# Keys and values loaded by pairs of batch rows, in a one-core decode block

## The chip, the cores and the metric

The kernel runs on one core of a Trainium2 chip. The metric is the device time of one execution in microseconds (us); lower is better. The traces are taken by the hardware profiler in one execution.

## The reference

One decode step (one token for each of 4 batch rows) of a transformer block: layer norm, attention over the last W = 2048 positions of a key and value cache, a residual, a second layer norm and a gated feed-forward network. All tensors are bf16.

```python
B, D, F = 4, 1024, 3584
Hq, Hkv, Sk, Dh = 32, 4, 8192, 128        # 8 query heads share one key head
W = min(4096, max(256, Sk // 4))          # 2048

def _A_ref(x, k_cache, v_cache, wq, wo):
    q = (x @ wq).reshape(B, 1, Hq, Dh).transpose(0, 2, 1, 3)
    k = jnp.repeat(k_cache[:, :, Sk - W:, :], 8, axis=1)
    v = jnp.repeat(v_cache[:, :, Sk - W:, :], 8, axis=1)
    scores = jnp.einsum("bhqd,bhkd->bhqk", q, k) * (Dh ** -0.5)
    p = _softmax(scores, axis=-1)
    o = jnp.einsum("bhqk,bhkd->bhqd", p, v)
    return o.transpose(0, 2, 1, 3).reshape(B, 1, Hq * Dh) @ wo

def _B_ref(x, w1, w3, w2):
    return (_silu(x @ w1) * (x @ w3)) @ w2

h = x + _A_ref(_layernorm(x), k_cache, v_cache, wq, wo)
return h + _B_ref(_layernorm(h), w1, w3, w2)
```

## The kernel before

**The ring.** All weights, keys and values live in one SBUF tile, `ring`, of five units of 16384 elements per partition. wq takes units 0 and 1; the keys `k_s` units 3 and 4; the values of batch rows 0 and 1 unit 2, and of rows 2 and 3 unit 0, after wq. wo takes units 3 and 4 after the keys; w1 starts at unit 1 and reaches into unit 2, over the values; w3 starts at unit 3, over wo; the parts of w2 take unit 0 and then unit 1. Each load is one `dma_start` on SP's queue (`load`, line 124). SP issues in program order, and a load that reuses space waits until the last instruction that reads the overlapped bytes is done. The order is wq in three parts, keys, values, wo, w1, w3, w2 in five parts.

**Keys and values.** A row of the cache tensor is split over partitions: each of 32 pieces of 64 positions of each of the 4 key heads takes one partition, so a load of one batch row is 2 MB in rows of 16 KB per partition (`k_v`, line 75). There are four such loads for keys and four for values.

**Scores.** `transpose_k` turns the 64 blocks of 128x128 of one batch row on TensorE (line 267, PE), 16 at a time into PSUM, and copies them back over the keys, on VectorE (line 269, DVE) and ScalarE (line 271, ACT) in turn. `scores` (line 290) multiplies 32 query columns with 512 keys at a time, four such matmuls side by side in four column groups of the array, 16 per batch row. The keys of one head are every fourth column of the transposed blocks; that is the step of `kT` (line 285).

**Softmax and output.** `row_max` and `bias_of` give the maxima for a pair of batch rows, `softmax` (line 331) the exponentials on ACT, [128, 512] for each row. `spread` (line 344) multiplies each probability with a mask of four columns, one for each key head (`gmask`), so that a probability stands in the column of its head and zeros in the other three; `transpose_p` (line 366) transposes the 128x2048 result on DVE in 32x32 blocks into `PT`; `output` (line 381) multiplies it with the values in 16 matmuls that each take four blocks, and keeps the right parts with `jmask` (`od`, line 389); two additions on GpSimd (POOL, lines 398 and 399) follow. After the last row the outputs are gathered (`on_ps`, line 441; `oP`, line 448) and multiplied with wo (`y_ps`, line 468).

**The rest.** The second layer norm follows, `up_projection` of w1 (`gate`, line 492), the reciprocal for silu (line 513), `up_projection` of w3 (`up`), and two stages with w2 (lines 533 and 548).

The program's order is written out by hand (`manual_schedule`), so on each engine the instructions run in the order of the text.

Of the kernel before, what the change touches and what calls it, by code (L numbers as in the profile page):

```python
# [10 lines left out]
P = 128  # L11
# [3 lines left out]
BF16 = mybir.dt.bfloat16  # L15
FP32 = mybir.dt.float32
# [5 lines left out]
def kernel(  # L22
# [20 lines left out]
    nc = tc.nc  # L43

    B, _, D = A_x.shape
    Hkv, Sk, Dh = A_k_cache.shape[1], A_k_cache.shape[2], A_k_cache.shape[3]
# [3 lines left out]
    W = min(4096, max(256, Sk // 4))  # L50
# [4 lines left out]
    C = 4  # L55
    R = 32
    S = R // B
    DQ = D // C
# [7 lines left out]
    x_flat = A_x.flatten_outer_dims()  # L66
    out_flat = out.flatten_outer_dims()
    wq_v = A_wq.rearrange("(p kc) n -> p kc n", kc=KC)
    T = NQ // P
    JR = W // R  # L70
    L5 = R // Hkv
    JB = 16
    JM = 4

    k_v, v_v = (
        a[:, :, Sk - W : Sk, :].rearrange("b g (i j) d -> i g b (j d)", j=JR)
        for a in (A_k_cache, A_v_cache)
    )
    wo_v = A_wo.rearrange("(p t) n -> p (t n)", t=T)
# [6 lines left out]
    ktpool = ctx.enter_context(tc.tile_pool(name="ktpool", bufs=2))  # L86
    ptpool = ctx.enter_context(tc.tile_pool(name="ptpool", bufs=3))
    stream = ctx.enter_context(tc.tile_pool(name="stream", bufs=1))
    ps = ctx.enter_context(tc.tile_pool(name="ps", bufs=1, space=bass.MemoryType.PSUM))
# [8 lines left out]
    def at(unit, *shape):  # L98
        o = unit * UNIT
        view = ring[:, o : o + int(np.prod(shape))]  # L100
        if len(shape) == 1:
            return view
        names = "abc"[: len(shape)]
        return view.rearrange(
            f"p ({' '.join(names)}) -> p {' '.join(names)}", **dict(zip(names, shape))
        )

    wq_s = at(0, KC, NQ)
    k_s = at(3, B, JR, Dh)
    v_s = [at((2, 0)[b // 2], 2, JR, Dh)[:, b % 2] for b in range(B)]  # L110
    wo_s = at(3, T, D)
    w1_s = at(1, KC, F)
    w3_s = at(3, KC, F)
# [2 lines left out]
    o = 0  # L116
    for i, n in enumerate(W2B):
        if i == 1:
            o = UNIT
# [3 lines left out]
    def load(dst, src):  # L123
        nc.sync.dma_start(out=dst, in_=src)

    def load_values(i):
        for b in (2 * i, 2 * i + 1):
            load(v_s[b].rearrange("p j d -> p (j d)"), v_v[:, :, b])

    ctx.enter_context(tc.manual_schedule())  # L130


    x_nat = act.tile([P, DQ], BF16)
    nc.gpsimd.memset(x_nat[:], 0.0)
    nc.scalar.dma_start(out=x_nat[::S, :], in_=x_flat.rearrange("b (c n) -> c b n", c=C))
    for r in (slice(0, 1), slice(1, KC // 2), slice(KC // 2, KC)):
        load(wq_s[:, r, :], wq_v[:, r, :])
    for b in range(B):
        load(k_s[:, b].rearrange("p j d -> p (j d)"), k_v[:, :, b])
    load_values(0)  # L140


# [15 lines left out]
        out=same[:], in_=t32[:].rearrange("p (o h) -> p o h", o=1).to_broadcast([P, C, R])  # L158
    )
    gmask = const.tile([P, 1, Hkv], BF16)  # L160
    with nc.allow_low_precision("sums of zeros and a single one"):
        nc.vector.tensor_reduce(
            out=gmask[:, 0], in_=t32[:].rearrange("p (g r) -> p g r", g=Hkv), axis=AX.X, op=ALU.add
# [3 lines left out]
    for j in range(JM):  # L167
# [3 lines left out]
        out=nscale[:], in_=ident_f[:2, :2], scalar=-qscale, op=ALU.mult  # L171
# [5 lines left out]
        out=place[:, : R * C].rearrange("p (h e) -> p h e", e=C)[:, :, C - 1], in_=t32[:]  # L177
# [6 lines left out]
        out=gather[:, :, :B], in_=ident[:].rearrange("p (c b s) -> p c b s", c=C, b=B)[:, :, :, 0]  # L184
# [44 lines left out]
    for kc in range(KC):  # L229
        for hf in range(2):  # L230
            for c in range(C):
                o = (2 * c + hf) * HALF * Dh
# [3 lines left out]
                    rhs=wq_s[:, kc, o : o + HALF * Dh],  # L236
                    start=(kc == 0),
                    stop=(kc == KC - 1),
# [6 lines left out]
    for r in range(REP):  # L245
# [8 lines left out]
        out=Qm[:].rearrange("p b (g y) -> p b g y", y=QW)[:, :, :, :REP],  # L254
        in_=qT_ps[:, :, :, :B].rearrange("p r g b -> p b g r"),
# [2 lines left out]

    n_step = 0

    def transpose_k(b, tags):
        nonlocal n_step
        for n in range(JR // JB):
            blocks = k_s[:, b, n * JB : (n + 1) * JB, :]
            kt_ps = ps.tile([P, JB, P], BF16, tag=tags[n_step % len(tags)], name="kt_ps")
            for jj in range(JB):
                nc.tensor.transpose(out=kt_ps[:, jj], in_=blocks[:, jj, :], identity=ident[:])  # L267
            if n_step % 2 == 0:
                nc.vector.tensor_copy(out=blocks, in_=kt_ps[:])  # L269
            else:  # L270
                nc.scalar.copy(out=blocks, in_=kt_ps[:])  # L271
            n_step += 1
# [4 lines left out]
    def scores_tile(i):  # L277
        sc_ps[i] = ps.tile([P, 2, W // C], FP32, tag=("scA", "scB")[i], name="sc_ps")
# [3 lines left out]
    om = act.tile([P, B, Dh], FP32)  # L282
    stage = {}

    kT = k_s.rearrange("p b j (q i g) -> p b g q j i", q=C, g=Hkv)

    def scores(b, gs):
        for g in gs:
            for q in range(C):
                nc.tensor.matmul(  # L290
                    sc_ps[b // 2][R * q : R * q + R, b % 2],
                    lhsT=Qm[:, b, g * R : (g + 1) * R],
                    rhs=kT[:, b, g, q],
                    start=(g == 0),
                    stop=(g == Hkv - 1),
                    tile_position=(0, R * q),
                )
# [40 lines left out]
        )  # L338
        stage[("p1", b)] = p1

    def spread(b):

        P4 = ktpool.tile([P, JR * L5, Hkv], BF16, tag="P4")
        nc.vector.tensor_tensor(  # L344
            out=P4[:],
            in0=stage.pop(("p1", b))[:].rearrange("p (x o) -> p x o", o=1).to_broadcast([P, JR * L5, Hkv]),
            in1=gmask[:].to_broadcast([P, JR * L5, Hkv]),
            op=ALU.mult,
        )
        stage[("P4", b)] = P4  # L350

    def total(i):

# [7 lines left out]
        )  # L361
        nc.vector.reciprocal(out=rinv[:, 2 * i : 2 * i + 2], in_=tot_ps)  # L362

    def transpose_p(b):
        PT = ptpool.tile([P, JR, R], BF16, tag="PT")
        nc.vector.transpose(  # L366
            out=PT[:].rearrange("p j h -> p (j h)"),
            in_=stage.pop(("P4", b))[:].rearrange("p x g -> p (x g)"),
        )
        stage[("PT", b)] = PT  # L370


    def output(b):
        PT = stage.pop(("PT", b))
        o_ps = (
            small[:, 0].rearrange("p (j d) -> p j d", j=JM)
            if b % 2
            else ps.tile([P, JM, Dh], FP32, tag="ktA", name="o_ps")[:]
        )
        for i in range(JR // JM):  # L380
            nc.tensor.matmul(  # L381
                o_ps,
                lhsT=PT[:, i * JM : (i + 1) * JM, :].rearrange("p j h -> p (j h)"),
                rhs=v_s[b][:, i * JM : (i + 1) * JM, :],
                start=(i == 0),
                stop=(i == JR // JM - 1),
            )
        od = act.tile([P, JM, Dh], FP32, tag="od", bufs=1)
        nc.vector.scalar_tensor_tensor(  # L389
            out=od[:],  # L390
            in0=o_ps,
            scalar=rinv[:, b : b + 1],
            in1=jmask[:].to_broadcast([P, JM, Dh]),
            op0=ALU.mult,
            op1=ALU.mult,
        )
        o2 = act.tile([P, 2, Dh], FP32, tag="o2", bufs=1)
        nc.gpsimd.tensor_tensor(out=o2[:], in0=od[:, :2], in1=od[:, 2:], op=ALU.add)  # L398
        nc.gpsimd.tensor_tensor(out=om[:, b], in0=o2[:, 0], in1=o2[:, 1], op=ALU.add)

    GS = range(Hkv)
    KT = ("ktA", "ktB", "scB")
    transpose_k(0, KT)
    transpose_k(1, KT)
    scores_tile(0)
    scores(0, GS)
    transpose_k(2, KT)
    scores(1, GS)
    transpose_k(3, KT)
    small = ps.tile([P, 2, 512], FP32, tag="ktB")  # L410
    scores_tile(1)
    scores(2, GS)
    row_max(0)
    scores(3, GS)
    bias_of(0)
    softmax(0)
    softmax(1)
    load(wo_s, wo_v.rearrange("p (t n) -> p t n", t=T))
    spread(0)
    row_max(1)  # L420
    transpose_p(0)
    bias_of(1)
    softmax(2)
    softmax(3)
    spread(1)
    transpose_p(1)
    total(0)
    output(0)
    spread(2)
    transpose_p(2)  # L430
    output(1)
    load(w1_s, w1_v)
    spread(3)
    transpose_p(3)
    total(1)
    output(2)
    output(3)

    on_ps = ps.tile([P, B, T], FP32, tag="scA")
    for e in range(C):  # L440
# [3 lines left out]
            rhs=om[:, :, e * T : (e + 1) * T],  # L444
            start=(e == 0),
            stop=(e == C - 1),
# [6 lines left out]
    for i in range(2):  # L453
        for k in range(2):
            c = i + 2 * k
# [3 lines left out]
                rhs=x_nat[:],  # L459
                start=(k == 0),  # L460
                stop=False,
# [3 lines left out]
    for t in range(T):  # L465
        row = wo_s[:, t].rearrange("p (k i n) -> p i k n", k=2, i=2)
        for i in range(2):
# [3 lines left out]
                rhs=row[:, i],  # L471
                start=False,
                stop=(t == T - 1),
# [34 lines left out]
    for w, n in zip(w2_s[1:], W2B[1:]):  # L508
# [8 lines left out]
        out=hg[:].rearrange("p (a f) -> p a f", a=2), in0=up_ps[:, :, :FH], in1=eg[:], op=ALU.mult  # L517
# [11 lines left out]
    for w, n in zip(w2_s[:NE], W2B[:NE]):  # L529
        for ff in range(n):  # L530
            row = w[:, ff].rearrange("p (k i n) -> p i k n", k=2, i=2)
            for i in range(2):
# [3 lines left out]
                    rhs=row[:, i],  # L536
                    start=(fc == 0),
                    stop=(fc == FE - 1),
# [6 lines left out]
    for w, n in zip(w2_s[NE:], W2B[NE:]):  # L545
        for ff in range(n):
            for c in range(C):
# [3 lines left out]
                    rhs=w[:, ff, c * DQ : (c + 1) * DQ],  # L551
                    start=(fc == FE),
                    stop=(fc == FC - 1),
# [5 lines left out]
    for i in range(2):  # L559
        for half, eng in enumerate((nc.sync, nc.scalar)):  # L560
            c = 2 * half + i
            eng.dma_start(
                out=out_flat[:, c * DQ : (c + 1) * DQ], in_=res[R * c : R * c + B, :]
# [31 lines left out]
```

## Time and profile before

| what | value |
|---|---|
| time, median of 3 runs | 139.23 us (139.12 to 139.4) |
| the profiled execution | 139.25 us |
| its span, first to last instruction | 137.2 us |
| PE, DVE, ACT, POOL busy | 55%, 36%, 21%, 11% of the span |
| SP's load queue | 55.58 MB, 95.0% of 16 DMA engines over the span |
| chain that ended last | DMA 60%, PE 27%, DVE 6%, ACT 3% |

Times are microseconds from the first instruction. PE is the matmul side of TensorE, PEld its weight loads; an engine's name with a q is its sequencer (SPq issues the loads). In a time line each row is: start, duration, engine, line, operation, output and inputs with shapes, count, and in brackets how long the engine was idle before and what ended it. In a list of waits: who waited for whom, the total, how often, the longest. "ring<-in_B_w_dram" is any of w1, w3 and w2. The page's row of DMA gives the busy tenths of the DMA engines in 40 equal slices of the span.

### The profile page before, as it was taken

What the parts mean: (1) busy time and instruction counts of PE and PEld (TensorE: products, weight loads), DVE (VectorE), ACT (ScalarE), POOL (GpSimd) and SP (SyncE); (2) the same over time, 40 slices, a digit from 0 to 9 for tenths busy, and PEclk for the clock granted to TensorE, in tenths of its full rate; (3) what the DMA queues carried; (4) which work ended last, traced back from release to release, by engine and by line L of the source; (5) the groups of instructions that cost most, each with busy time, mean ns of one, the idle gap of its engine ahead of it and who ended that gap; (6) DMA issues with size and microseconds to landing.
All of it is one profiled execution on the core that took longest, in us unless ns stands there. A gap on an engine that the chain in (4) does not pass through costs nothing.

```text
span 137.2 us, 1720 instructions
## 1 busy us (share of the span) xinstructions
PE 75.5 (55%) x744; PEld 41.4 (30%) x746; DVE 49.3 (36%) x47; ACT 28.5 (21%) x31; POOL 15.3 (11%) x41
## 2 busy tenths in 40 slices
PE   0002904689999983149938757971098000927450
PEld 0001301289875940033414314420043000404120
DVE  0012000016733563899699620023000297061021
ACT  3005000208949494022000000005001700000000
POOL 7304100000000000000358321002000000000000
PEclk9999995559999999555999999998556855699998
DMA  4999998999999999998979989969989899999950
GB/s 162 488 424 456 449 401 373 406 435 439 411 435 444 416 425 415 430 578 358 573 306 420 497 358 439 535 284 518 418 384 523 351 451 386 419 410 418 402 195 2
DMA packets 2795, 55.70 MB, mean 406 GB/s; under 512 B 324, under 2 KB 356, under 8 KB 612
## 3 DMA queue, kind: packets, MB, share of 16 engines
q1 hardware_dynamic: 2752, 55.58, 95.0%
q8 instruction: 6, 0.10, 0.3%
q10 hardware_dynamic: 36, 0.01, 0.0%
q14 instruction: 1, 0.01, 0.0%
HBM read 55.58 MB, written 0.01 MB: 405 GB/s over the span
## 4 chain that ended last, share of the span: by engine, by line
DMA 60%; PE 27%; DVE 6%; ACT 3%; issue 1%; SPq 1%; DVEq 0%
DMA ring<-in_B_w_dram 45%; DMA ring<-in_A_wq_dram 15%; PE kt_ps L267 9%; PE sc_ps L290 5%; PE o_ps L381 4%; PE gate L492 3%; PE q_ps L233 3%; DVE P L344 2%; DVE PT L366 2%; ACT ring L271 1%; PE small L381 1%; DVE ring L269 1%; DVE rmax L302 1%; PE qT_ps L246 1%; ACT q_sb L243 1%
## 5 line engine op out<-in xcount | busy, mean ns | idle before, releaser
L271 ACT COPY ring<-kt_ps 128x2048 bf16<-128x2048 bf16 x8 | 14.6, 1866 | 8.3 <-PE kt_ps L267 8.3
L267 PE MATMUL kt_ps<-ident,ring 128*128 128x128 bf16 x256 | 15.8, 225 | 0.6 <-DVE Qm L253 0.5
L267 PEld LDWEIGHTS <-ring 128*128 128x128 bf16 x256 | 15.3, 101 | 2.6 <-DMA ring<-in_A_k_cache_dram 1.7
L398 POOL TENSOR_TENSOR o<-od 128x256 f32<-128x256 f32 x4 | 6.8, 1696 | 59.7 <-DVE od L389 59.7
L269 DVE COPY ring<-kt_ps 128x2048 bf16<-128x2048 bf16 x8 | 9.8, 1225 | 10.1 <-PE kt_ps L267 10.1
L492 PEld LDWEIGHTS <-n_T 128*32 128x32 bf16 x128 | 4.7, 133 | 21.9 <-DMA ring<-in_B_w_dram 11.5
L233 PE MATMUL q_ps<-ring,n_T 128*32 128x512 bf16 x64 | 7.2, 627 | 7.2 <-DMA ring<-in_A_wq_dram 5.5
L513 DVE RECIPROCAL eg<-eg 128x896 f32<-128x896 f32 x1 | 5.8, 5753 | 13.2 <-ACT eg L512 13.2
L492 PE MATMUL up<-ring,n_T 128*32 128x448 bf16 x64 | 4.5, 452 | 10.8 <-DMA ring<-in_B_w_dram 10.8
L381 PEld LDWEIGHTS <-PT 128*128 128x128 bf16 x64 | 6.7, 108 | 9.2 <-issue 2.1
L344 DVE TENSOR_TENSOR P<-p,gmask 128x2048 bf16<-128x2048 bf16 x4 | 9.1, 2277 | 0.8 <-ACT p L331 0.8
L366 DVE STREAM_TRANSPOSE PT<-P 128x2048 bf16<-128x2048 bf16 x4 | 9.2, 2306 | 0.1
L492 PE MATMUL gate<-ring,n_T 128*32 128x448 bf16 x64 | 6.1, 574 | 5.5 <-DMA ring<-in_B_w_dram 5.5
L381 PE MATMUL o_ps<-ring,PT 128*128 128x512 bf16 x31 | 8.6, 431 | 0.2 <-issue 0.2
L193 PE MATMUL sums_ps<-both,mean_f 128*128 128x64 f32 x4 | 1.1, 367 | 13.0 <-ACT both L191 13.0
L290 PE MATMUL sc_ps<-ring,Qm 128*32 128x512 bf16 x64 | 7.6, 604 | 0.4 <-DVE ring L269 0.4
L533 PE MATMUL early_ps<-ring,hg_T 128*32 128x512 bf16 x42 | 4.9, 379 | 5.3 <-DMA ring<-in_B_w_dram 5.3
L381 PE MATMUL small<-ring,PT 128*128 128x512 bf16 x31 | 7.2, 379 | 0.7 <-DVE rinv L362 0.7
L468 PE MATMUL y_ps<-ring,oP 128*32 128x512 bf16 x64 | 7.1, 379 | 0.1
L233 PEld LDWEIGHTS <-n_T 128*32 128x32 bf16 x64 | 2.4, 139 | 11.2 <-issue 9.3
L253 DVE COPY Qm<-qT_ps 128x128 bf16<-128x128 bf16 x1 | 0.3, 292 | 15.0 <-PE qT_ps L246 15.0
L193 PEld LDWEIGHTS sums_ps<-both,mean_f 128*128 128x128 f32 x4 | 0.8, 250 | 13.5 <-issue 11.0
(77 smaller groups left out, 58.8 us busy)
## 6 DMA issues: line engine op xcount, KB each, us to landing
ring<-in_B_w_dram SPq DMA_DIRECT2D x2, 7168.0 KB
ring<-in_A_k_cache_dram SPq DMA_DIRECT2D x4, 2048.0 KB
ring<-in_A_v_cache_dram SPq DMA_DIRECT2D x4, 2048.0 KB, 43.0
ring<-in_A_wq_dram SPq DMA_DIRECT2D x1, 4096.0 KB, 20.7
ring<-in_B_w_dram SPq DMA_DIRECT2D x1, 3328.0 KB
ring<-in_A_wq_dram SPq DMA_DIRECT2D x1, 3072.0 KB, 11.5
ring<-in_B_w_dram SPq DMA_DIRECT2D x1, 2048.0 KB, 27.2
ring<-in_A_wq_dram SPq DMA_DIRECT2D x1, 1024.0 KB, 4.6
```

The costliest lines, as they stand in the source:

```text
L233: nc.tensor.matmul(q_ps[R * c : R * c + R, hf], lhsT=xn_T[:, kc, :], rhs=wq_s[:, kc, o : o + HALF * Dh], start=(kc == 0), stop=(kc == KC - 1),
L267: nc.tensor.transpose(out=kt_ps[:, jj], in_=blocks[:, jj, :], identity=ident[:])
L269: nc.vector.tensor_copy(out=blocks, in_=kt_ps[:])
L271: nc.scalar.copy(out=blocks, in_=kt_ps[:])
L290: nc.tensor.matmul(sc_ps[b // 2][R * q : R * q + R, b % 2], lhsT=Qm[:, b, g * R : (g + 1) * R], rhs=kT[:, b, g, q], start=(g == 0), stop=( ...
L344: nc.vector.tensor_tensor(out=P4[:], in0=stage.pop(("p1", b))[:].rearrange("p (x o) -> p x o", o=1).to_broadcast([P, JR * L5, Hkv]), in1=g ...
L366: nc.vector.transpose(out=PT[:].rearrange("p j h -> p (j h)"), in_=stage.pop(("P4", b))[:].rearrange("p x g -> p (x g)"),)
L381: nc.tensor.matmul(o_ps, lhsT=PT[:, i * JM : (i + 1) * JM, :].rearrange("p j h -> p (j h)"), rhs=v_s[b][:, i * JM : (i + 1) * JM, :], star ...
L398: nc.gpsimd.tensor_tensor(out=o2[:], in0=od[:, :2], in1=od[:, 2:], op=ALU.add)
L468: nc.tensor.matmul(y_ps[R * i : R * i + R], lhsT=oP[:, t, :], rhs=row[:, i], start=False, stop=(t == T - 1), tile_position=(0, R * i), ski ...
L492: nc.tensor.matmul(out_ps[R * c : R * c + R, hf, :FH], lhsT=hn_T[:, kc, :], rhs=w[:, kc, o : o + FH], start=(kc == 0), stop=(kc == KC - 1) ...
L513: nc.vector.reciprocal(out=eg[:], in_=eg[:])
```

## The change

Keys and values are loaded by pairs of batch rows: 16 pieces of 128 positions of each of 8 (batch row, head) combinations, one piece per partition, in rows of 32 KB. So there are two key loads and two value loads of 4 MB. A 128x128 block now holds the keys of two batch rows, and one head's keys of one row are every eighth column. `transpose_k` works on halves of a pair (64 blocks each).

A probability now belongs in one of eight columns, two batch rows by four heads. `spread` writes the four columns of its own row; the other four are zeros, set once by GpSimd in two tiles `P4`, one for even and one for odd rows. A row's probabilities are handled in two halves, so there are eight spreads of 1024 elements, eight transposes of 2048 and eight groups of 16 output matmuls. w1's load stands in the text after both halves of row 1's output.

The input x is loaded in five transfers instead of one.

```diff
-    JR = W // R
-    L5 = R // Hkv
+    PB = 2
+    GP = PB * Hkv
+    JR = W * GP // P
+    LP = R // GP
+    NH = 2
+    JH = JR // NH
...
-        a[:, :, Sk - W : Sk, :].rearrange("b g (i j) d -> i g b (j d)", j=JR)
+        a[:, :, Sk - W : Sk, :].rearrange("(m b) g (i j) d -> i (b g) m (j d)", b=PB, j=JR)
...
-    k_s = at(3, B, JR, Dh)
-    v_s = [at((2, 0)[b // 2], 2, JR, Dh)[:, b % 2] for b in range(B)]
+    k_s = at(3, B // PB, JR, Dh)
+    v_s = [at(u, JR, Dh) for u in (2, 0)]
...
-    nc.scalar.dma_start(out=x_nat[::S, :], in_=x_flat.rearrange("b (c n) -> c b n", c=C))
+    for c, rows in ((0, (0, 2)), (0, (2, B)), (1, (0, B)), (2, (0, B)), (3, (0, B))):
+        nc.scalar.dma_start(
+            out=x_nat[R * c + S * rows[0] : R * c + S * rows[1] : S, :],
+            in_=x_flat[rows[0] : rows[1], c * DQ : (c + 1) * DQ],
+        )
...
-    for b in range(B):
-        load(k_s[:, b].rearrange("p j d -> p (j d)"), k_v[:, :, b])
+    for m in range(B // PB):
+        load(k_s[:, m].rearrange("p j d -> p (j d)"), k_v[:, :, m])
...
-    kT = k_s.rearrange("p b j (q i g) -> p b g q j i", q=C, g=Hkv)
+    kT = k_s.rearrange("p m j (q i b g) -> p m b g q j i", q=C, b=PB, g=Hkv)
...
-    def spread(b):
-        P4 = ktpool.tile([P, JR * L5, Hkv], BF16, tag="P4")
+    P4 = [ktpool.tile([P, JH * LP, PB, Hkv], BF16, name="P4") for _ in range(PB)]
+    for z in range(PB):
+        nc.gpsimd.memset(P4[z][:, :, 1 - z, :], 0.0)
+
+    def spread(b, h):
         nc.vector.tensor_tensor(
-            out=P4[:],
...
+            out=P4[b % PB][:, :, b % PB, :],
+            in0=stage[("p1", b)][:, h * JH * LP : (h + 1) * JH * LP]
...
-    def transpose_p(b):
-        PT = ptpool.tile([P, JR, R], BF16, tag="PT")
+    def transpose_p(b, h):
+        PT = ptpool.tile([P, JH, R], BF16, tag="PT")
         nc.vector.transpose(
             out=PT[:].rearrange("p j h -> p (j h)"),
-            in_=stage.pop(("P4", b))[:].rearrange("p x g -> p (x g)"),
+            in_=P4[b % PB][:].rearrange("p x b g -> p (x b g)"),
...
-        for i in range(JR // JM):
+        for i in range(JH // JM):
+            j = h * JH + i * JM
             nc.tensor.matmul(
                 o_ps,
                 lhsT=PT[:, i * JM : (i + 1) * JM, :].rearrange("p j h -> p (j h)"),
-                rhs=v_s[b][:, i * JM : (i + 1) * JM, :],
-                start=(i == 0),
-                stop=(i == JR // JM - 1),
+                rhs=v_s[b // PB][:, j : j + JM, :],
+                start=(j == 0),
+                stop=(j == JR - JM),
             )
+        if h < NH - 1:
+            return
...
-    transpose_k(0, KT)
-    transpose_k(1, KT)
+    transpose_k(0, 0, KT)
+    transpose_k(0, 1, KT)
     scores_tile(0)
     scores(0, GS)
-    transpose_k(2, KT)
+    transpose_k(1, 0, KT)
     scores(1, GS)
-    transpose_k(3, KT)
+    transpose_k(1, 1, KT)
...
+    spread(0, 0)
     row_max(1)
-    transpose_p(0)
+    transpose_p(0, 0)
     bias_of(1)
     softmax(2)
     softmax(3)
-    spread(1)
-    transpose_p(1)
+    spread(0, 1)
+    transpose_p(0, 1)
     total(0)
-    output(0)
-    spread(2)
-    transpose_p(2)
-    output(1)
+    output(0, 0)
+    spread(1, 0)
+    transpose_p(1, 0)
+    output(0, 1)
+    spread(1, 1)
+    transpose_p(1, 1)
+    output(1, 0)
+    spread(2, 0)
+    transpose_p(2, 0)
+    output(1, 1)
     load(w1_s, w1_v)
-    spread(3)
-    transpose_p(3)
     total(1)
-    output(2)
-    output(3)
+    spread(2, 1)
+    transpose_p(2, 1)
+    output(2, 0)
+    spread(3, 0)
+    transpose_p(3, 0)
+    output(2, 1)
+    spread(3, 1)
+    transpose_p(3, 1)
+    output(3, 0)
+    output(3, 1)
```

## Prediction before the change was run

> **What bounds the kernel now.** I read the page first (the span in slices, the chain that ended last), then what the SP queue waited for, then the time lines of PE, DVE and SP. The profiled execution took 139.25 us (median 139.23) with a span of 137.2; 2.05 us lie outside it, and I leave them as they are. This measurement can tell about 0.2%, 0.28 us, from no change.
>
> ```profile
> DMA  4999998999999999998979989969989899999950
> ...
> 68.29 31.25 DMA ring<-in_B_w_dram
> 99.67 3.91 PE gate L492 x37
> 103.58 0.10 SPq L124
> 103.72 30.02 DMA ring<-in_B_w_dram
> ```
>
> The second row of the page and three steps of the chain: the 16 DMA engines are full from 2 us to the end, and the chain consists mostly of weights arriving. So the time is the time of one unbroken stream of 55.58 MB, as long as SP issues each load before the one ahead of it has drained. A load that reuses space of the ring first waits for the last reader of that space:
>
> ```profile
> SPq L124 <- PE small L381: 14.8, 1, 14.8
> SPq L124 <- DMA ring<-in_A_wo_dram: 14.0, 1, 14.0
> SPq L124 <- PE y_ps L468: 8.3, 1, 8.3
> ...
> 68.29 0.33 SPq L124 DMA_DIRECT2D ring<-in_B_w_dram  x1
> 90.90 0.80 SPq L124 DMA_DIRECT2D ring<-in_B_w_dram  x2
> ```
>
> The waits of SP's queue, then SP's time line around two of them. w1 is issued at 68.29 when half of `output(1)` has read the values. w3, with the first part of w2 behind it, is issued at 90.90 when `y_ps` has read the part of wo that w3 covers. In the packet records w1's packets start at 80.19, and they end at 97.1 on the first DMA engine and 99.1 on the last. So w3 is 6.2 us early. **That slack is what the change has to pay from**, and `y_ps` ends the chain scores, softmax, spread, transpose, output:
>
> ```profile
> 28.66 4.56 PE L267 MATMUL kt_ps<-ident,ring 128*128 128x128 bf16 x64 [0.45 <-DVE Qm L253]
> 37.05 1.89 PE L290 MATMUL sc_ps<-ring,Qm 128*32 128x512 bf16 x16
> 46.37 3.65 ACT L271 COPY ring<-kt_ps 128x2048 bf16<-128x2048 bf16 x2 [1.85 <-PE kt_ps L267]
> 53.73 2.29 DVE L344 TENSOR_TENSOR P<-p,gmask 128x2048 bf16<-128x2048 bf16 x1 [0.85 <-ACT p L331]
> 66.37 3.62 PE L381 MATMUL small<-ring,PT 128*128 128x512 bf16 x16
> 69.55 2.31 DVE L366 STREAM_TRANSPOSE PT<-P 128x2048 bf16<-128x2048 bf16 x1
> 84.64 7.08 PE L468 MATMUL y_ps<-ring,oP 128*32 128x512 bf16 x64
> ```
>
> From the time lines of PE, ACT and DVE: the durations of this chain's steps, which the sum below uses.
>
> **Keys by pairs: when the chain starts.** Today the transposes start at 28.66, behind Qm; the first 2 MB of keys landed at 27.1. The first pair is 4 MB; the packets of today's second load end at 31.93, so the first transposes start about 0.4 us behind that (wq's last packet ended at 22.09, its matmul started at 22.46): 32.35. Longer rows give little: a 16 KB row takes 614 ns, wq's 32 KB row 1213, so each engine saves 15 ns on each of 32 rows, 0.5 us in all. If one transfer were cut into 16 KB packets anyway, only that would go. PE idles from 28.2 to 32.35, so its granted clock, 0.50 in 25 to 30, stays low. Around 28.7 the 128-wide transposes started 107 ns apart at that clock, later 56 ns. Half-clock stretches end 3.2 us (61.3 to 64.6) after steady work returns; with the idle part of a window ahead I take 4.9 us: 46 slow transposes, 18 quick ones, 5.95 us. (A clock that recovers at once: 3.75.)
>
> **The scores' reads.** kT's inner step becomes 8 elements, 16 bytes, instead of 4. The trace has no matmul with such a step. Lower bound: today's, four 512-column matmuls in 0.432 us. That is already 0.83 ns a column, against 0.42 for the contiguous rows of `y_ps` (one matmul per 0.108 us, two side by side). Upper bound: twice, 0.86. The nearest rows of 16 bytes are DVE's `x_T` (256 elements at that step) and `hg_T` (896 at 56 bytes):
>
> ```profile
> L218 DVE STREAM_TRANSPOSE x_T<-x_nat x1: 627/627/627, 9.8 to 9.8; 128x256 bf16<-128x256 bf16 x1
> L218 DVE STREAM_TRANSPOSE hg_T<-hg x1: 1700/1700/1700, 122.2 to 122.2; 128x896 bf16<-128x896 bf16 x1
> ```
>
> Line L218's groups, ns min/median/max: 1073 ns for 640 more elements, 1.68 ns each, where the contiguous 2048 of L366 took about 1.03 above the same fixed part. 1.68 is also twice the scores' 0.83, as if a new 16-byte piece each 1.67 ns were the limit and today's step drew two columns from it. I take the upper end: 3.53 us for 16 matmuls instead of 1.82. [...]
>
> **Two new waits.** `scores(0)` now needs both halves of pair 0, and PE stands behind it in order. The last block of a half is copied by ACT: two copies in 3.65 us, the last one ending 1.9 us after its transposes (48.1 to 50.0). So 1.95 us before scores(0), and the same before scores(2), where 0.42 is waited now. Behind each is all of PE's work.
>
> Start 32.35 + 5.95 + 3.75 (second half) + 1.95 + 3.53 + 3.75 + 3.53 + 3.73 + 1.95 + 3.53 + 0.1 + 3.52 = 67.65 for the end of scores(3); the second pair, at about 43, is in time. The spread then starts 1.36 us later as now (52.37 to 53.73): **69.0 instead of 53.73, +15.3**.
>
> **Spread, transpose, output.** Eight spreads of 1024 elements instead of four of 2048, 1.21 us each (2.28 less 1024 elements at 1.04 ns); the 8-byte pieces stay contiguous, and I charge the written step nothing (bounds: 1.14 and, at 1.68 ns an element, 1.9). Eight transposes of 2048 at 2.31 instead of four: +9.2 us of DVE. 128 matmuls instead of 64, 3.6 us per 16 at the full clock: +14.5 of PE. They chase each other. From the first spread: spread, maximum, its matmul and first transpose 5.9; total 0.7; output(0,0) 5.9 (cold, 5.2 now), output(0,1) 3.6, od 0.8: 16.9. DVE waits for that od, then spread and transpose (1,1) 3.5, output(1,1) 3.7, od 0.8, total and reciprocal 0.6: 25.5. (2,1) and (3,0) on DVE 7.0, with PE beside; od 1.1; (3,1) 3.5; its output 3.7: **40.8 instead of 27.0, +13.8**.
>
> From the last output to w3's issue stays 10.1 us (80.77 to 90.90): reduction on POOL, on_ps, oP, and y_ps as far as w3 covers wo. w3 issues at 69.0 + 40.8 + 10.1 = 119.9. First packets follow 1.0 us later (the first load: issue 0.73, packet 1.77): 120.9. Today w3's first packet flows at 97.1. What follows w3 in the stream is unchanged. **Stream's shift: 120.9 - 97.1 = 23.8; 139.25 + 23.8 = 163.0.**
>
> **What costs nothing, and its cover.** wo waits for scores(3): issued at 67.7, though the values drain near 60.5, so the stream has a hole of 8 us; it lands near 89, and y_ps wants it at 113. w1 waits for half of output(1,1), 22 us after the first spread: 91, landing near 110, and the gate wants it at 125, after the layer norm (4.1 us behind y_ps). Both holes lie inside the shift and count once. The gate's exponent, reciprocal and product end near 141, `up` near 144.5, so w3 still ends last there. The five x transfers hold ACT for up to 5 x 1.1 us; one x row now travels per packet of wq (0.93 us apart), so x may land at 15 instead of 9.8. The first half of q then ends near 23; the second waits for wq until 22.4 anyway, and the keys' wait until 32 covers the rest. Without these covers it would cost 5. The POOL memsets of zeros (1024 elements, 0.95 us by oP's) run at 14 to 17, while POOL idles until 67. SP has four issues fewer.
>
> **Rivals.**
> - Scores keep 0.432 us per four (one element a read, whatever the step): 4 x 1.71 = 6.8 less, **156.2**. For it: 0.83 ns is also just half the contiguous rate. Chance 0.22.
> - The spread's strided writes cost 1.9 us: six of the eight on the path, +4, **167**. Chance 0.07.
> - Pair rows slow the stream. Neighbouring pieces of a pair lie 8 MB apart in memory; today's four heads are 2 MB apart and run at 26.7 bytes per ns and engine. At half rate the first pair lands 10 us later and the second 19: the scores then end near 82 and the time is near **177**. [...] Chance 0.04.
> - The other side: the stream hides all, and the rows' 0.5 us remain: **138.8**. This decides itself at w3's issue: it holds only if w3 leaves by 96, 5 us later than now. Against it, DVE's 9.2 us of added transposes and the 3.7 us later start alone bring 104. Chance 0.04.
> - The forecast: 0.63; its own range is 160 to 166 (clock back at once: 160.8; a longer first output).
>
> The range takes in the first rival and its quick clock (154): 154 to 166. Chances: faster 0.03, same 0.01, slower 0.96.
>
> **What would show it.** First transposes of keys near 32.4; 16 scores in 3.5 us (1.8 would make the first rival right); 1.9 us of PE waiting for ACT's copy before scores(0) and (2); eight DVE pairs of 1.2 and 2.3 us; w3's issue near 120, and DMA slices below 5 around 61 to 68 and 110 to 121. A w3 issued before 96 would prove the forecast wrong.

## Result and the profile after

The changed kernel takes 182.73 us (median of 6, 181.55 to 183.17) against 139.32: 1.3109 times as long, with an interval of 1.3087 to 1.3131. The forecast was 163.0, in a range of 154 to 166: the sign was right, the size too small by 20 us. Some executions of e8 and e12 below ran in a slower state, and their times are left out.

The page's two rows of the DMA engines, slices of 4.5 us. The first is the busy share, the second what was moved; the third row is that of the kernel before, in slices of 3.4 us:

```profile
DMA  5998997999997999979999999979999799899970
GB/s 217 450 480 377 449 225 152 210 225 232 225 221 152 210 228 225 225 159 221 210 232 217 268 449 435 438 317 533 419 419 371 292 471 469 349 424 407 415 296 5
...
GB/s 162 488 424 456 449 401 373 406 435 439 411 435 444 416 425 415 430 578 358 573 306 420 497 358 439 535 284 518 418 384 523 351 451 386 419 410 418 402 195 2
```

The engines look as busy as before. But from the sixth slice to the twenty-second, 22 to 101 us, they move 152 to 232 GB/s, mostly 210 to 232: about half of what they move ahead of it and behind it, and of what the kernel before moves in the same loads. This is exactly while keys and values arrive: a 32 KB row of a pair takes 2.55 us, where a 32 KB row of wq in the same execution takes 1.21 (medians of the packet records, which hold start, duration and size of each transfer of a DMA engine; a row is one such packet). So the four pair loads take 79.6 us of the stream instead of 39.2. The busy share, 7 to 9 tenths in these slices, does not show the slowed transfers; the row of GB/s does.

From the chain that ended last (start, duration, what):

```profile
5.59 37.61 DMA ring<-in_A_k_cache_dram
...
43.25 6.15 PE kt_ps L274 x64
...
53.33 1.88 ACT ring L278
...
55.24 3.60 PE sc_ps L297 x15
58.84 5.34 another core or an unknown queue
...
64.23 5.89 PE kt_ps L274 x64
```

The first key transposes start at 43.25, not 32.4, as the first pair's last packet ends at 42.4. After scores(0) PE waits again, for the second pair, whose last packet ends at 63.4 (the page calls these 5.34 us unknown; PE's time line names the key load). The rest looks as foreseen:

```profile
55.24 3.60 PE L297 MATMUL sc_ps<-ring,Qm 128*32 128x512 bf16 x16 [1.95 <-ACT ring L278]
64.23 5.89 PE L274 MATMUL kt_ps<-ident,ring 128*128 128x128 bf16 x64 [5.39 <-DMA ring<-in_A_k_cache_dram]
...
87.88 1.23 DVE L354 TENSOR_TENSOR P<-p,gmask 128x1024 bf16<-128x1024 bf16 x1 [0.84 <-ACT p L338]
91.52 2.29 DVE L377 STREAM_TRANSPOSE PT<-P 128x2048 bf16<-128x2048 bf16 x1
```

Time lines of PE and DVE: 16 scores in 3.60 us after 1.95 us of waiting for ACT's copy, spreads of 1.2 us, transposes of 2.3. The first spread starts at 87.88, the last output ends at 128.80, and w3's first packet starts at 139.90.

### The profile page after: what moved, and what is told of

It is laid out like the page before. It is cut to its first block, busy times and chain, and to the rows that moved or that the text cites. A ratio compares the mean times of both kernels' runs of the same rounds, so it can differ in the third digit from the quotient of the medians.

```text
span 180.8 us, 1854 instructions
## 1 busy us (share of the span) xinstructions
PE 102.0 (56%) x807; PEld 51.3 (28%) x810; DVE 59.2 (33%) x55; ACT 28.7 (16%) x31; POOL 15.8 (9%) x43
## 4 chain that ended last, share of the span: by engine, by line
DMA 40%; PE 36%; DVE 12%; ACT 5%; another core or an unknown queue 3%; issue 2%; POOL 1%; SPq 0%; POOLq 0%; DVEq 0%; ACTq 0%
DMA ring<-in_A_k_cache_dram 21%; DMA ring<-in_B_w_dram 16%; PE kt_ps L274 9%; PE sc_ps L297 8%; PE o_ps L395 7%; DVE PT L377 5%; ACT ring L278 4%; PE small L395 4%; PE y_ps L497 4%; DMA ring<-in_A_wq_dram 3%; DVE P L354 3%; PE gate L521 2%; DVE od L405 2%; PE on_ps L470 1%
## 5 line engine op out<-in xcount | busy, mean ns | idle before, releaser
L274 PE MATMUL kt_ps<-ident,ring 128*128 128x128 bf16 x256 | 19.5, 252 | 20.3 <-DMA ring<-in_A_k_cache_dram 20.2
L274 PEld LDWEIGHTS <-ring 128*128 128x128 bf16 x256 | 18.9, 117 | 24.2 <-DMA ring<-in_A_k_cache_dram 22.2
L377 DVE STREAM_TRANSPOSE PT<-P 128x2048 bf16<-128x2048 bf16 x8 | 18.5, 2309 | 0.3
L395 PEld LDWEIGHTS <-PT 128*128 128x128 bf16 x128 | 12.9, 104 | 19.6 <-DVE PT L377 4.0
L395 PE MATMUL o_ps<-ring,PT 128*128 128x512 bf16 x63 | 16.6, 422 | 0.6 <-DVE PT L377 0.4
L297 PE MATMUL sc_ps<-ring,Qm 128*32 128x512 bf16 x64 | 14.4, 1031 | 3.9 <-ACT ring L278 3.9
L395 PE MATMUL small<-ring,PT 128*128 128x512 bf16 x62 | 14.4, 379 | 1.9 <-DVE PT L377 1.8
L354 DVE TENSOR_TENSOR P<-p,gmask 128x1024 bf16<-128x1024 bf16 x8 | 9.8, 1221 | 0.8 <-ACT p L338 0.8
L521 PEld LDWEIGHTS <-n_T 128*32 128x32 bf16 x128 | 4.4, 136 | 17.9 <-DMA ring<-in_B_w_dram 10.7
L338 ACT ACTIVATE p<-sc_ps,bias 128x512 bf16<-128x512 f32 x4 | 2.7, 684 | 23.2 <-DVE P L354 16.7
```

Of the source, the lines that this page charges most:

```text
L297: nc.tensor.matmul(sc_ps[b // 2][R * q : R * q + R, b % 2], lhsT=Qm[:, b, g * R : (g + 1) * R], rhs=kT[:, b // PB, b % PB, g, q], start=(g ...
L354: nc.vector.tensor_tensor(out=P4[b % PB][:, :, b % PB, :], in0=stage[("p1", b)][:, h * JH * LP : (h + 1) * JH * LP] .rearrange("p (x o) -> ...
L377: nc.vector.transpose(out=PT[:].rearrange("p j h -> p (j h)"), in_=P4[b % PB][:].rearrange("p x b g -> p (x b g)"),)
L395: nc.tensor.matmul(o_ps, lhsT=PT[:, i * JM : (i + 1) * JM, :].rearrange("p j h -> p (j h)"), rhs=v_s[b // PB][:, j : j + JM, :], start=(j ...
L521: nc.tensor.matmul(out_ps[R * c : R * c + R, hf, :FH], lhsT=hn_T[:, kc, :], rhs=w[:, kc, o : o + FH], start=(kc == 0), stop=(kc == KC - 1) ...
```

## Experiments: what halves the loads

Two theories came first. *Outer count*: the source of a pair load has 16 outer pieces (of 8 rows), the load before had 32 (of 4); with 16, by this theory, each DMA engine fills eight partitions in a row, and that halves the rate. *Addresses*: the two batch rows of a pair lie 8 MB apart in memory, the third rival of the prediction. In e1 to e4 and in e8 to e10 keys or values are other ones, or in other places, than the reference's. Row times are medians of the packet records. e1, e2, e4, e9, e10 and e11 ran once each; the kernel before stayed within 139.05 to 139.92 in all its executions beside these runs.

**e1_sixteen_outer**, the kernel before:

```diff
-        a[:, :, Sk - W : Sk, :].rearrange("b g (i j) d -> i g b (j d)", j=JR)
+        a[:, 0].rearrange("b (s i j) d -> i s b (j d)", s=8, j=JR)
```

> Edit of the kernel before: same loads of 2 MB, same 16 KB rows, but the source is walked as 16 outer pieces of 8 rows (one whole head, rows 256 KB apart inside a piece) instead of 32 outer pieces of 4; keys and values are other ones than the reference's. Outer-count theory (with 16 outer pieces each DMA engine fills eight partitions in a row, and the stream halves whatever the addresses): a 16 KB row takes about 1.27 us instead of 0.614, the key and value loads 20 us per 4 MB, the time is near 179.5 (the stream alone is 40 longer). Address theory (the two batch rows of a pair lie 8 MB apart in memory, and such rows collide): nothing here is 8 MB apart, rows stay at 0.614 us and the time at 139.3.

179.75 us; 16 KB rows 1.28 us instead of 0.614:

```profile
GB/s 216 465 435 420 417 203 210 232 203 214 221 199 225 199 214 203 210 236 192 221 203 210 365 417 325 443 457 415 413 426 452 490 443 426 342 443 395 419 307 12
```

So neither pairs, nor 32 KB rows, nor 8 MB are needed. With the old work on the compute engines, halving the rate of these loads costs 40.4 us.

**e4_32_outer_8mb**, the kernel before:

```diff
-        a[:, :, Sk - W : Sk, :].rearrange("b g (i j) d -> i g b (j d)", j=JR)
+        a[:, :, Sk - W : Sk, :].rearrange("b g (i j) d -> i b g (j d)", j=JR)
```

> Edit of the kernel before: each 2 MB load takes one head of all four batch rows, so the four rows of a piece lie 8 MB apart, with 32 outer pieces as before; keys and values land in other places than the reference's. Outer-count theory: 0.614 us a row and 139.3. Address theory: rows near 1.27 us, time near 179.

139.18 us; rows 0.614. All rows of a piece are 8 MB apart and nothing is lost: the address theory falls.

**e2_no_8mb**, the changed kernel, with the eight rows of a piece 512 KB apart:

```diff
-        a[:, :, Sk - W : Sk, :].rearrange("(m b) g (i j) d -> i (b g) m (j d)", b=PB, j=JR)
+        a[:PB, :2].rearrange("m g (s i j) d -> i (g s) m (j d)", s=4, j=JR)
```

> Edit of the changed kernel: the eight rows of a piece are 512 KB apart in two heads that follow each other, not in two batch rows 8 MB apart; still 16 outer pieces of 32 KB rows; keys and values are other ones than the reference's. Outer-count theory: 2.55 us a row, time near 182.7 as changed. Address theory: 1.21 us a row and, with the added work of the change only, near 163.

182.04 us; rows 2.56. The same answer from the other side. Rows of a piece that are 256 KB (e1), 512 KB (e2) or 2 MB apart (the changed kernel, within a batch row) are slow with 16 outer pieces; 2 MB (the kernel before) and 8 MB (e4) are quick with 32.

**e3_in_one_piece**, the changed kernel (with the index of the loads to match):

```diff
-        a[:, :, Sk - W : Sk, :].rearrange("(m b) g (i j) d -> i (b g) m (j d)", b=PB, j=JR)
+        a[:PB, :2].rearrange("m g (i j) d -> (g i) m (j d)", j=JR)
```

> Edit of the changed kernel: each pair load reads 4 MB in one piece, 128 rows of 32 KB one after another; keys and values are other ones than the reference's. Both theories: 1.21 us a row, and the rest of the prediction stands alone: 163.0 (160 to 166), first key transposes at 32.4, first spread at 69, third weight load near 120. If a 4 MB load of 32 KB rows is slow by itself, 182.7.

163.95 us (162.86 to 165.07; 1.1799 times before, 1.1717 to 1.1881); rows 1.22. It splits the loss: 18.8 us come from the half rate, 24.6 from the added work and waits. Rows of its page and time lines:

```profile
DMA  5999999999999990297996759990066999799960
...
32.44 5.09 PE L274 MATMUL kt_ps<-ident,ring 128*128 128x128 bf16 x64 [6.08 <-DMA ring<-in_A_k_cache_dram]
43.38 3.60 PE L297 MATMUL sc_ps<-ring,Qm 128*32 128x512 bf16 x16 [1.95 <-ACT ring L278]
...
68.60 1.23 DVE L354 TENSOR_TENSOR P<-p,gmask 128x1024 bf16<-128x1024 bf16 x1 [0.85 <-ACT p L338]
```

Both holes of the forecast are there, in the 16th and 17th slices and the 28th and 29th (4 us each).

Then: what does the outer count do? A *memory* theory: 16 streams with such addresses are too many. An *in-step* theory: some engines slow one another while they are in step. *In step* means here that the engines are at the same row of their own pieces.

**e9_eight_outer** and **e10_two_outer**, the kernel before, with the source of e1 but `s=16` and `s=64`:

```diff
-        a[:, :, Sk - W : Sk, :].rearrange("b g (i j) d -> i g b (j d)", j=JR)
+        a[:, 0].rearrange("b (s i j) d -> i s b (j d)", s=16, j=JR)    # e10: s=64
```

> Edit of the kernel before: key and value loads of 2 MB walked as 8 outer pieces of 16 rows, other keys and values. [...] Memory theory (16 streams with such addresses are too many for the memory): with 8 streams 0.614 us a row, 9.8 us a load, 179.

> Edit of the kernel before: key and value loads of 2 MB walked as 2 outer pieces of 64 rows, other keys and values. [...] Rival (any source with fewer than 32 outer pieces makes each row slow): 1.27 us a row, 81 us a load, near 750.

252.12 and 443.97 us. e10's rows take 0.614 us, and its page moves 53 GB/s, two engines' worth at 26.7 bytes per ns: two pieces kept two engines at work, and a small count is not slow by itself. e9's first load has rows of 1.26 us at 110 GB/s, so eight streams are slowed as sixteen are, against the memory theory; but its rows quicken, to a median of 0.755 in the fifth load, and slow down again later. Eight engines at e1's 1.28 us a row would take 20.5 us a load and 264 in all, two at 0.614 would take 39.3 and 414 (estimates, with 4.9 us a load and 139.3 in the kernel before). The times miss them since rows quicken in e9, and since wo overlaps the last values in e10: there 64 KB rows of wo take 4.70 us, against 2.42 before, although only two engines still carry values, and the rows of these two go from 0.614 in the seventh load to 1.18 in the eighth.

If engines slow one another only when they are in step, putting them out of step must help, with source and addresses untouched.

**e11_stagger_four**, the changed kernel, a load ahead of the keys:

```diff
+    load(
+        v_s[0].rearrange("p j d -> p (j d)")[80:96],
+        A_k_cache[0, 1, : 4 * 4 * JR].rearrange("(s i j) d -> i s (j d)", s=4, j=JR),
+    )
     for m in range(B // PB):
```

> Edit of the changed kernel: ahead of the first key load, one load of 4 outer pieces of 4 rows of 32 KB into value space that is not yet in use; only the first four DMA engines take part, so they are four rows behind the next four from then on. Pair loads, their addresses and their 16 outer pieces as changed. [...]

194.71 us. If four pieces take four engines, as two took two in e10, the added load leaves four engines four rows behind the other twelve (an estimate), and some rows of the pair loads should be quick. None are: all stay near 2.56, as they would if source or addresses made a row slow by themselves, a miss for the theory as it was put. But while the added rows run, rows take 3.65 us, three times 1.22 (all 16 rows that start between 25 and 30 us). That the slowest engines set the pace for all would fit this and the slow rows of e10; no run shows it by itself.

**e12_stagger_all**, e11 and one more load ahead of it:

```diff
+    pad = v_s[0].rearrange("p j d -> p (j d)")
+    load(
+        pad[32:80],
+        A_k_cache[0, 0, : 12 * 4 * JR].rearrange("(s i j) d -> i s (j d)", s=4, j=JR),
+    )
```

> [...] Address or outer-count theory: all rows near 2.5 us and 183 to 190.

183.47 us, one execution; the page's second row of DMA:

```profile
GB/s 215 450 492 376 434 231 210 159 210 347 462 441 365 448 430 332 278 116 29 231 462 462 448 246 202 396 405 405 215 0 4 405 406 430 438 417 417 421 307 4
```

Half rate in the sixth to ninth slices (23 to 41 us), while the added loads run beside the first keys; from then on rows of 1.22 to 1.26 us (medians of each 5 us from 40 to 85), with the very source that takes 2.55 in the changed kernel. **The half rate belongs neither to the source nor to its addresses by themselves: the same loads run at the full rate behind the added ones.** By the estimate above, twelve pieces and then four leave four engines eight rows behind, eight engines four rows, and four none. That engines in step slow one another fits this, and remains an inference: no record names an engine, and out of step the engines also read other addresses at the same moment. Which engines meet, and where, no run shows. e3's 163.95 and eight added rows of 1.21 us would make 173.6 (an estimate). The time is longer, since the added rows ran at half rate as well: first key transposes at 52.83, 20.4 us behind e3's, and the profiled execution 20.6 us behind e3's (162.86).

## Experiments: the added work

**e5_eight_byte_step**, on top of e3:

```diff
-    kT = k_s.rearrange("p m j (q i b g) -> p m b g q j i", q=C, b=PB, g=Hkv)
+    kT = k_s.rearrange("p m j (q b i g) -> p m b g q j i", q=C, b=PB, g=Hkv)
```

> Edit of the run with the loads in one piece: the scores read every fourth column of a block again (8 bytes apart) instead of every eighth, with the same number of columns; the columns are then partly those of the other batch row. Forecast's theory (a step of 16 bytes doubles the scores): 16 scores in 1.82 us instead of 3.60, four times, 7.1 us less on the chain, about 156.5 against 163.6 without. Rival (the scores are slow for another reason, the clock or the order of the halves): 3.6 us and no change.

157.07 us (156.55 to 157.59), 6.9 less than e3. From PE's time line:

```profile
43.66 1.89 PE L297 MATMUL sc_ps<-ring,Qm 128*32 128x512 bf16 x16 [1.95 <-ACT ring L278]
```

1.89 us at a step of 8 bytes, 3.60 at 16, with all else alike: the step is the cause.

**e6_output_part_alone**, the kernel before with the changed kernel's `P4`, `spread`, `transpose_p`, `output` and their order; both halves of a row are multiplied with the same values:

```diff
+    PB = 2
+    NH = 2
+    JH = 64
+    LP = 4
...
                 rhs=v_s[b][:, i * JM : (i + 1) * JM, :],
-                start=(i == 0),
-                stop=(i == JR // JM - 1),
+                start=(j == 0),
+                stop=(j == NH * JH - JM),
```

> Edit of the kernel before: only spread, transpose and output as in the change (eight spreads of 1024 with four columns of zeros, eight transposes, 128 output matmuls); loads, keys, scores as before. Both halves are multiplied with the same values, so the output is another sum. Forecast's theory: first spread at 53.7 as before, last output 40.8 later, third weight load issued at 104.6, first packet 105.6 against 97.1 when the queue drains: 139.3 + 8.5 = 147.8. Rival (the stream hides it): 139.3.

147.91 us (147.13 to 148.69; 1.0623 times, 1.0491 to 1.0756). w3's first packet starts at 105.90 (forecast 105.6), w1's first engine is done at 97.3: a hole of 8.6 us, and the time is 8.7 longer (9.4 in the profiled execution, 148.69, where the hole stands).

**e7_x_in_five**, the kernel before with the five transfers of x:

```diff
-    nc.scalar.dma_start(out=x_nat[::S, :], in_=x_flat.rearrange("b (c n) -> c b n", c=C))
+    for c, rows in ((0, (0, 2)), (0, (2, B)), (1, (0, B)), (2, (0, B)), (3, (0, B))):
+        nc.scalar.dma_start(
...
```

> Edit of the kernel before: only x in five transfers. Forecast: x lands 2 to 5 us later, covered by the wait for the query weights; 139.3, no change. Rival (queries late, first key transposes late by what x lost): first key transposes at 29 to 32 and still no change, since third weight load has 6 us to spare.

139.49 us, 1.0010 times (0.9999 to 1.0022). q's first matmul starts at 17.67 instead of 13.40, and the first key transposes at 28.52 as ever: covered.

**e8_keys_4mb_alone**, the kernel before with two key loads of 4 MB:

```diff
-    for b in range(B):
-        load(k_s[:, b].rearrange("p j d -> p (j d)"), k_v[:, :, b])
+    for m in range(2):
+        load(
+            k_s[:, 2 * m : 2 * m + 2].rearrange("p b j d -> p (b j d)"),
+            A_k_cache[m, :2].rearrange("g (i j) d -> (g i) (j d)", j=2 * JR),
+        )
```

> Edit of the kernel before: only the key loads are 4 MB each (in one piece, so at the full rate; other keys). Forecast: first transposes at 32.4 instead of 28.7, slow clock a little longer, first spread near 58.5, third weight load issued near 95.7 where the queue drains at 97.1: all of it inside the 6.2 us to spare, 139.1 to 139.4. Rival (the later start counts in full): 143 to 144.

140.27 us (median of five, 139.93 to 141.68), 1.0093 times (1.0058 to 1.0129): a small loss, where 139.1 to 139.4 was expected. The profiled one (139.97) comes nearest to the forecast: first transposes at 32.42, first spread at 58.36, w3 issued at 95.99 where w1's packets are through on the first engine at 97.10, so 1.1 us early and no hole before w3. With so little to spare, a chain that is a little later shows in the time. Which step was late in the longer executions no trace shows; the granted clock, which stood at 0.818 in the one of 141.68 and at 0.860 to 0.866 in the other four, is a guess.

## Why the prediction was wrong, and where it was right

**The step that failed** is the price of a pair's row, in "Keys by pairs: when the chain starts". I took 1213 ns from wq's 32 KB rows: the right size, but wq's source has 128 equal rows and a pair's has 16 pieces of 8. Measured: 2.55 us. The step "the first transposes start at 32.35" became 43.25, and "the second pair, at about 43, is in time" became a wait of 5.4 us until 64.2. With it the first spread came at 87.88 instead of 69.0 and w3's first packet at 139.90 instead of 120.9: 19.0 of the 19.7 us that are missing.

**The third rival** named a half rate and gave 177, with a chance of 0.04 and the wrong cause: by e4, rows 8 MB apart cost nothing, with 0.614 us a row. No run shows that such a distance halves the rate; the runs showed it for loads of 16 outer pieces (2.55 us a row instead of 1.21, and 2.56 in e2 with rows 512 KB apart). So the nearness of 177 to the result is luck in part. The sum of the rival was short as well. The scores ended at 86.5, not near 82: the second pair landed 21 us later than in e3, not 19, and its transposes took 5.89 us instead of 3.75, with a granted clock of 0.62 from 65 to 70 us. And the rival left out the values: the stream by itself, with them at half rate too, comes to 179.75 (e1). In the changed kernel stream and chain end almost together: w1's packets are through on the first engine at 138.90, and w3's start at 139.90. So the holes in the stream, which make up the forecast's shift of 23.8 us, shrank to 1.0 ahead of w3, filled by the slow loads.

**What stays open.** 2.55 is twice and 3.65 three times 1.22, and behind the added loads of e12 the rows run at 1.22; no record names an engine, so that engines in step are the cause is an inference. That a few of them slow all engines is my reading of e11 and e10, and was not tested alone; the quickening in e9 was not followed up.

**Right, by e3,** where only the half rate is taken away: 163.95 against 163.0. First transposes 32.44 (forecast 32.35); 3.53 us from scores(0) to the next transposes, 43.38 to 46.91 (3.53); ACT's copy 1.95 (1.95); first spread 68.60 (69.0); 40.7 from there to the end of the last output (40.8); w3's first packet 120.33 (120.9). The slow clock after the wait was 0.9 us shorter than charged (5.09 for 64 transposes instead of 5.95; in the changed kernel itself 6.15, with a granted clock of 0.50 from 40 to 45 us and 0.67 from 45 to 50). The first rival, scores at the old rate, falls by e5; its price of 6.8 was right (6.9). The second, dear strided writes, falls by the spreads' 1.2 us. The fourth, the stream hides all, falls by e6.

**The covers**: x's later landing is free (e7). The later start of the keys was nearly free, as the 6.2 us to spare allowed: it costs 1.0 us in the median (e8), more than the 0.2 at most that was expected.

No run here beats the kernel before: with the loads at full rate the pairs still bring twice the output work and slower scores.

## What to carry to other kernels

Price a load by a row that has the same outer structure, not only the same bytes: a source with 16 pieces of 8 rows ran at half the rate of one with 32 of 4 (16 KB rows in 1.28 us in e1, 0.614 in e4), or of one with 128 rows one after another (32 KB rows in 2.55 us, 1.22 in e3), while the busy share stayed at 7 to 9 tenths. So look at the GB/s beside it. In a kernel that is bound by one stream of loads, find for each load by how much it is issued before the queue drains; that slack, 6.2 us here, is what any longer chain is paid from, and what lies beyond it counted in full (a hole of 8.6 us cost 8.7 in e6).

## What was not expected of the hardware

- The same pair loads run at three rates: 32 KB rows take 2.55 us in the changed kernel, 3.65 while a small load of four pieces runs beside them (e11), and 1.22 behind two small loads (e12); wq's and e3's rows of that size take 1.21 and 1.22. That engines in step slow one another is inferred from this.
- The slowing seems to take in all engines, which is inferred as well: all rows are at 2.56 in e11, where by the estimate four engines are out of step with the rest, and wo's rows take 4.70 instead of 2.42 in e10, beside two engines that carry values.
- The number of engines went with the number of outer pieces where that was below 16: 2 pieces moved 53 GB/s with rows of 0.614 us, so two engines; 8 at first 110 with rows of 1.26, so about eight.
